# Filling the attention stage's idle TensorE time with 512-token blocks read back from DRAM instead of 288-token halves kept in SBUF

## The chip, the cores and the metric

The program runs on one core of a Trainium2 chip. A core has five engines, each with its own in-order instruction stream: TensorE (PE; its weight loads are shown as PEld), VectorE (DVE), ScalarE (ACT), GpSimd (POOL) and SyncE (SP), which here issues all DMAs. The metric is the device time of one execution in microseconds, lower is better. The kernel before took 1243.93 us (median of three executions, 1243.01 to 1246.9).

## The reference, cut to what matters

Three layers follow each other on a batch of 8 sequences of 576 tokens with 512 channels.

```python
# 1. attention over 32 pooled memories: 8 batches x 8 heads, phi [.., 576, 32]
a   = softmax(phi, over the 576 tokens' 32 memories)
k_m = einsum('bhsm,bhsd->bhmd', a, k);  v_m = the same with v
x   = softmax(q @ k_m.T / 8) @ v_m                 # [8, 576, 512]
# 2. mixer: tokens, then channels
h = relu(x.T @ w_tok1) @ w_tok2;   u = x + h.T     # w_tok1 576x256, w_tok2 256x576
x = u + relu(u @ w_ch1) @ w_ch2                    # w_ch1 512x1536, w_ch2 1536x512
# 3. four experts of causal attention (64 wide), top 2 of 4 by a gate, weighted sum
out = sum over e of gate[e] * softmax(mask(q_e @ k_e.T / 8)) @ v_e @ wo[e]
```

All results are float32. The mixer's weights come as 64-bit floats and are turned into 32-bit words on the chip.

## The kernel before, in words

Every large product is made from three passes over a high and a low part (`mm3`, line 93): a value x is split into hi, a rounded copy made by ACT, and lo = x - hi, made by DVE (`split`, line 100).

The first stage ("stage A", lines 197 to 578) does attention and the token mixer for 16 units, a unit being four heads of one batch. It is a software pipeline: in iteration t of the loop at line 540 the functions `s1a` ... `s4c` each work on another unit, from t+3 down to t. `s2k` (line 294) pools k and v with `kv` as its operand and writes `ks` and the values; `s4g`, `s4b` and `s4c` are the token mixer of unit t. `s4c` writes a result tile u, which ACT takes out of PSUM (line 472), and stores it to DRAM as `u_d` (line 475). The channel mixer's 1536 hidden channels are 12 chunks (`fc`) of 128. Chunks 0 to 2 are computed in stage A as fill between the pieces of the pipeline, 7 to 10 us of TensorE work for each iteration; they read u from the tile in SBUF (`u1`), in halves of 288 tokens, 16 halves in all. A half (`block_1`, line 188) is four splits, three `mm1_1` (12 matmuls each) and four `mm2_1` (9 matmuls each), whose sum is added to u and stored as `p_d`. What is not done when stage A ends is done at the head of the second stage.

The second stage ("stage B", lines 602 to 720) reads u back from `u_d` (tiles `ub`) in 9 blocks of 512 tokens, computes chunks 3 to 9, adds the stored `p_d` (tiles `pb`) and stores `x_d`. The third stage computes chunks 10 and 11 and the experts' attention. The 64-bit weights of a chunk come in two tensors; each is one DMA of 512 KB (tile `cst`), five DVE operations and two ACT operations (`f64_split`, line 111). `N1 + NP` chunks are prepared in stage A, the rest in stage B by `chload` (line 674). `go()` puts one such step at a time into the pipeline, `fill(k)` some pieces of fill.

The code's order is not the final one: a scheduler reorders the instructions of every engine when the program is built, so the order of each engine's instructions is shown below where it matters. At run time each engine goes through its stream in order and waits by semaphores. A DMA that SP issues waits on SP, and what stands behind it waits as well.

## Time and profile before

| | |
|---|---|
| three executions | 1243.01, 1243.93, 1246.9 us |
| profiled execution, its own time | 1243.78 us |
| its span, from first to last instruction | 1242.1 us |
| mean granted TensorE clock | 0.996 |
| PE, PEld busy | 1197.0 us, 1103.0 us |
| DVE, ACT, POOL busy | 703.5, 593.1, 382.5 us |
| DMA | 142.93 MB, 115 GB/s on average |

A profile has views: the page (busy shares, slices, the chain that ended last, costliest groups), stretches of time with each engine's busy time, groups of instructions of one form, the instructions in order of time, and DMA issues with their time to landing. Busy time of PE overstates its work, since a matmul's end is modelled and matmuls overlap; the distance between the starts of two neighbours is what one costs. In the list by time a bracket gives the idle time before an instruction and whose result ended it.

### The profile page before, as it was taken

How to read it: one execution, taken by the hardware profiler on the slowest of the kernel's cores; microseconds unless marked ns; L12 is line 12 of the kernel's file. 1: busy time of each engine (PE TensorE's matmuls, PEld its weight loads, DVE VectorE, ACT ScalarE, POOL GpSimd, SP SyncE). 2: the span in 40 equal slices, each digit the busy share in tenths (PEclk: the TensorE clock that was granted, in tenths of full speed). 3: DMA queues.
4: the chain of work that ended last, by engine and by line, in shares of the span. 5: the costliest groups of instructions: out<-in, count | busy, mean ns of one | idle time of the engine just before them, and what ended most of it. 6: DMA issues, size and time to landing. Idle time of an engine off the chain costs nothing. (4 is left out here: it accounts for less than half of the span.)

```text
span 1242.1 us, 22995 instructions
## 1 busy us (share of the span) xinstructions
PE 1197.0 (96%) x8460; PEld 1103.0 (89%) x8460; DVE 703.5 (57%) x1757; ACT 593.1 (48%) x1542; POOL 382.5 (31%) x588
## 2 busy tenths in 40 slices
PE   5799999999999999999999999999999999999997
PEld 4789999999999888888888888999999999998995
DVE  6877576776546743222222214776666766676754
ACT  3555364655534411111111113676676767675775
POOL 1443242433300142000000006446363627282322
PEclk9899999999999999999999999999999999999999
DMA  9886574645218455320321104222223323331421
GB/s 231 231 212 177 149 186 140 179 135 143 78 68 295 134 156 178 102 72 30 102 69 68 57 37 111 61 82 79 80 85 82 97 66 109 98 88 46 136 92 60
DMA packets 159615, 142.93 MB, mean 115 GB/s; under 512 B 73104, under 2 KB 128400, under 8 KB 159504
## 3 DMA queue, kind: packets, MB, share of 16 engines
q1 hardware_dynamic: 159504, 141.47, 39.3%
q8 instruction: 67, 1.10, 0.4%
q14 instruction: 44, 0.36, 0.1%
HBM read 90.05 MB, written 39.85 MB: 105 GB/s over the span
## 5 line engine op out<-in xcount | busy, mean ns | idle before, releaser
L627 DVE SCALAR_TENSOR_TENSOR hl<-h,hh 128x512 fp32r<-128x512 f32 x63 | 43.4, 691 | 225.7 <-ACT hh L626 225.6
L626 ACT ACTIVATE hh<-h 128x512 fp32r<-128x512 f32 x63 | 37.5, 597 | 255.3 <-PE h L98 255.3
L923 POOL TENSOR_TENSOR a<-a,cf 128x128 f32<-128x128 f32 (+3 forms) x128 | 88.0, 720 | 62.3 <-DVE cf L915 50.9
L98 PE MATMUL h<-uh,w1h 128*128 128x512 f32 x252 | 98.0, 390 | 0.4 <-DVE hl L627 0.4
L98 PE MATMUL h<-ul,w1h 128*128 128x512 f32 x252 | 98.1, 389 | 0.0
L98 PE MATMUL o<-hl,w2h 128*128 128x512 f32 x252 | 98.1, 389 | 0.0
L98 PE MATMUL o<-hh,w2l 128*128 128x512 f32 x252 | 98.0, 389 | 0.0
L98 PE MATMUL h<-uh,w1l 128*128 128x512 f32 x252 | 98.0, 389 | 0.0
L98 PE MATMUL o<-hh,w2h 128*128 128x512 f32 x252 | 88.9, 389 | 0.0
L867 DVE CUSTOM_DVE_ANT_0 ssb<-s,cmask 128x128 f32<-128x128 f32 (+2 forms) x144 | 69.3, 484 | 31.6 <-PE s L878 20.5
L389 POOL TENSOR_TENSOR at<-ssb,ssm 128x640 f32<-128x640 f32 x16 | 21.4, 1336 | 200.3 <-DVE ks L316 110.8
L880 ACT ACTIVATE a<-ssb,nb 128x128 f32<-128x128 f32 (+3 forms) x128 | 71.5, 559 | 13.8 <-DVE nb L867 8.8
L98 PE MATMUL g<-xl,qkh 128*128 128x288 f32 x256 | 76.4, 299 | 0.0
L98 PE MATMUL g<-xh,qkh 128*128 128x288 f32 x256 | 75.7, 301 | 0.2 <-DVE kk L803 0.2
L98 PE MATMUL g<-xh,qkl 128*128 128x288 f32 x256 | 75.6, 296 | 0.0
L729 POOL MEMSET cmask<- 128x640 f32 x1 | 0.6, 632 | 226.0 <-PE h L98 226.0
L780 POOL TENSOR_TENSOR xl<-p,xh 128x288 fp32r<-128x288 f32 x64 | 50.8, 809 | 45.1 <-ACT xh L779 45.1
L105 DVE TENSOR_TENSOR Bl<-t,Bh 128x512 fp32r<-128x512 f32 (+1 forms) x80 | 50.6, 635 | 18.8 <-ACT Bh L102 17.6
L98 PE MATMUL b<-uh,w1h 128*128 128x288 f32 x192 | 58.7, 306 | 0.0
L98 PE MATMUL b<-hh,w2h 128*128 128x288 f32 x192 | 58.4, 304 | 0.0
L98 PE MATMUL b<-hl,w2h 128*128 128x288 f32 x192 | 58.0, 302 | 0.0
L939 PE MATMUL t<-ident,a 128*128 128x128 f32 x320 | 55.7, 279 | 1.9 <-DVE Al L105 1.2
(261 smaller groups left out, 3998.9 us busy)
## 6 DMA issues: line engine op xcount, KB each, us to landing
cst<-in_moe_w_ch_dram SPq DMA_DIRECT2D x24, 512.0 KB, 4.7
u_d<-u SPq DMA_DIRECT2D x32, 288.0 KB, 2.2
p_d<-u SPq DMA_DIRECT2D x16, 576.0 KB, 3.3
ub<-u_d SPq DMA_DIRECT2D x9, 1024.0 KB, 5.2
pb<-p_d SPq DMA_DIRECT2D x36, 256.0 KB, 3.7
x_d<-pb SPq DMA_DIRECT2D x36, 256.0 KB, 2.4
u<-u_d SPq DMA_DIRECT2D x16, 576.0 KB, 4.3
p<-x_d SPq DMA_DIRECT2D x16, 576.0 KB, 4.1
```

Of the source, the lines that this page charges most:

```text
L98: PE.matmul(ps, lhsT=a, rhs=b, start=start and i == 0, stop=stop and i == len(seq) - 1)
L105: DVE.tensor_sub(lo, src, f(hi))
L389: POOL.tensor_mul(a_[:].rearrange("p j (h m) -> p j h m", h=4), s[:], sm[:, :, :, None].to_broadcast([128, 5, 4, M]))
L626: ACT.activation(hh[:], p[:], AF.Relu)
L627: DVE.scalar_tensor_tensor(hl[:], p[:], 0.0, f(hh[:]), op0=OP.max, op1=OP.subtract)
L729: POOL.memset(cmask[:], 0.0)
L780: POOL.tensor_sub(xl[b][:, c, ss], x_, f(xh[b][:, c, ss]))
L867: DVE.tensor_tensor_reduce(out=out, in0=p, in1=mask, scale=-scale, scalar=least, op0=OP.add, op1=OP.min, accum_out=acc)
L880: ACT.activation(a[:, aoff[c]:aoff[c] + W], s_[:, 0:W], AF.Exp, scale=-1.0, bias=nb[:, 0:1], accum_out=sm[:, c:c + 1])
L923: POOL.tensor_mul(x_, x_, cf[:, c:c + 1].to_broadcast([128, W]))
L939: PE.transpose(p[:, 128 * kc:128 * kc + 128], a[:, aoff[c] + 128 * kc:aoff[c] + 128 * kc + 128], ident[:])
```

## The change: what it does

The fill of stage A takes blocks of 512 tokens, 9 in all, instead of 16 halves of 288. It no longer reads u from SBUF: a block is loaded from `u_d` (`load_1`) once the unit that completes its 512 tokens has been stored, and its splits stand between the `mm2_1` of the block before. Fill starts at iteration 4 instead of 3, and a piece is given out for every second slot. The sum of chunks 0 to 2 is stored alone, by piece of 128 channels (tiles `po`), taken out of PSUM by ACT and DVE in turn; u is added to it in stage B by POOL, in `load_p`. One chunk's weights less are prepared in stage A and one more in stage B (`NP` 3), and the channel weights begin an iteration later. The masked values (`s2v`) are made one iteration later than the rest of `s2k`.

```diff
--- before.py
+++ after.py
@@ -130,7 +130,7 @@
         yield
 
 
-    N1, NP, N3 = 3, 4, 2
+    N1, NP, N3 = 3, 3, 2
     KM = KF - N3
     wch_ctx, b1_ctx, stg_ctx = ExitStack(), ExitStack(), ExitStack()
     wbm = wch_ctx.enter_context(tc.tile_pool(name="wbm", bufs=1, reuse_waits="tile"))
@@ -155,43 +155,66 @@
                                  l_[fc][:].rearrange("p c f -> p (c f)"), DM, wd)
 
 
-    u1, uh1, ul1, h1 = {}, {}, {}, {}
-
-    def half(j):
-        return slice(SH * (j % 2), SH * (j % 2) + SH)
-
-    def split_1(j, k0):
-        if k0 == 0:
-            uh1[j] = wk1.tile([128, KD, SH], F32R, name="uh1")
-            ul1[j] = wk1.tile([128, KD, SH], F32R, name="ul1")
-        split(uh1[j][:, k0, :], ul1[j][:, k0, :], u1[j // 2][:, k0, half(j)])
-
-    def mm1_1(j, fc):
-        p = ppb1.tile([128, SH], F32, name="b", bufs=2)
-        mm3(p[:], [((w1h[fc][:, kd, :], w1l[fc][:, kd, :]), (uh1[j][:, kd, :], ul1[j][:, kd, :]))
-                   for kd in range(KD)])
-        hh = wk1.tile([128, SH], F32R, name=f"hh{fc}")
-        hl = wk1.tile([128, SH], F32R, name=f"hl{fc}")
+    NBLK = NT // 512
+    ub1, uh1, ul1, h1 = {}, {}, {}, {}
+    units_out, split_out = -1, -1
+
+    def load_1():
+
+        k0 = len(ub1)
+        if k0 < NBLK and split_out >= k0 - 1 and units_out >= 2 * ((512 * k0 + 511) // S) + 1:
+            ub1[k0] = wk1.tile([128, KD, 512], F32, name="ub1")
+            SP.dma_start(ub1[k0][:], u_d[:, 512 * k0:512 * k0 + 512].rearrange("(c p) s -> p c s", p=128))
+
+    def split_1(k0, kd):
+        nonlocal split_out
+        if kd == 0:
+            uh1[k0] = wk1.tile([128, KD, 512], F32R, name="uh1")
+            ul1[k0] = wk1.tile([128, KD, 512], F32R, name="ul1")
+        split(uh1[k0][:, kd, :], ul1[k0][:, kd, :], ub1[k0][:, kd, :])
+        if kd == KD - 1:
+            split_out = k0
+            load_1()
+
+    def mm1_1(k0, fc):
+        p = ppb1.tile([128, 512], F32, name="b", bufs=2)
+        for i in range(2):
+            mm3(p[:], [((w1h[fc][:, kd, :], w1l[fc][:, kd, :]), (uh1[k0][:, kd, :], ul1[k0][:, kd, :]))
+                       for kd in range(2 * i, 2 * i + 2)], start=(i == 0), stop=(i == 1))
+            if i == 0:
+                yield
+        hh = wk1.tile([128, 512], F32R, name=f"hh{fc}")
+        hl = wk1.tile([128, 512], F32R, name=f"hl{fc}")
         ACT.activation(hh[:], p[:], AF.Relu)
         DVE.scalar_tensor_tensor(hl[:], p[:], 0.0, f(hh[:]), op0=OP.max, op1=OP.subtract)
-        h1[j, fc] = hh, hl
-
-    def mm2_1(j, c):
-        p = ppb1.tile([128, SH], F32, name="b", bufs=2)
-        mm3(p[:], [((w2h[fc][:, c, :], w2l[fc][:, c, :]), (h1[j, fc][0][:], h1[j, fc][1][:]))
+        h1[k0, fc] = hh, hl
+        yield
+
+    def mm2_1(k0, c):
+        p = ppb1.tile([128, 512], F32, name="b", bufs=2)
+        mm3(p[:], [((w2h[fc][:, c, :], w2l[fc][:, c, :]), (h1[k0, fc][0][:], h1[k0, fc][1][:]))
                    for fc in range(N1)])
-        u_ = u1[j // 2][:, c, half(j)]
-        DVE.tensor_add(u_, u_, p[:])
-        if c == KD - 1:
-            SP.dma_start(p_d[:, SH * j:SH * j + SH].rearrange("(c p) s -> p c s", p=128), u1[j // 2][:, :, half(j)])
-
-    def block_1(j):
-        for kd in range(KD):
-            yield split_1(j, kd)
+        o_ = wk1.tile([128, 512], F32, name="po1", bufs=2)
+        if c % 2:
+            DVE.tensor_copy(o_[:], p[:])
+        else:
+            ACT.activation(o_[:], p[:], AF.Copy)
+        SP.dma_start(p_d[128 * c:128 * c + 128, 512 * k0:512 * k0 + 512], o_[:])
+
+    def block_1(k0):
+        if k0 == 0:
+            while k0 not in ub1:
+                yield
+            for kd in range(KD):
+                yield split_1(k0, kd)
         for fc in range(N1):
-            yield mm1_1(j, fc)
+            yield from mm1_1(k0, fc)
+        while k0 + 1 < NBLK and k0 + 1 not in ub1:
+            yield
         for c in range(KD):
-            yield mm2_1(j, c)
+            if k0 + 1 < NBLK:
+                split_1(k0 + 1, c)
+            yield mm2_1(k0, c)
 
 
     with ExitStack() as sa:
@@ -227,7 +250,7 @@
         units = [(b, g) for b in range(B) for g in range(2)]
         NU = len(units)
         NR = 6
-        et, kmT, Vh, Vl, ah, al, pmc, est, kst, ssb, aTt, gt_, ht, pmx, Vd = ({} for _ in range(15))
+        et, kmT, Vh, Vl, ah, al, pmc, est, kst, ssb, aTt, gt_, ht, pmx, Vd, vmt = ({} for _ in range(16))
 
         def load_phi(n):
             b, g = units[n]
@@ -315,13 +338,16 @@
             kst[n] = ks
             DVE.scalar_tensor_tensor(ks[:], p[:, None, 0:64].to_broadcast([128, 2, 64]), r[:],
                                      kmask[:], op0=OP.mult, op1=OP.mult)
-            vm = wk_.tile([128, 64], F32, name="vm", bufs=1)
+            vm = wk_.tile([128, 64], F32, name="vm", bufs=2)
+            vmt[n] = vm
             ACT.activation(vm[:], p[:, 64:128], AF.Copy, scale=r[:])
             if n + 1 < NU:
                 load_kv(n + 1)
-            vmb = vm[:, None, :].to_broadcast([128, 4, 64])
-            h_ = wk_.tile([128, 4, 64], F32R, name="Vh", bufs=3)
-            l_ = wk_.tile([128, 4, 64], F32R, name="Vl", bufs=3)
+
+        def s2v(n):
+            vm = vmt.pop(n)
+            h_ = wk_.tile([128, 4, 64], F32R, name="Vh", bufs=2)
+            l_ = wk_.tile([128, 4, 64], F32R, name="Vl", bufs=2)
             Vh[n], Vl[n] = h_, l_
             vh = wk_.tile([128, 64], F32R, name="vh", bufs=1)
             vl = wk_.tile([128, 64], F32, name="vl", bufs=1)
@@ -332,7 +358,7 @@
             if n < NR:
                 Vd[n] = h_, l_
                 return
-            d_ = wk_.tile([128, 2, 4, 64], F32R, name="Vd", bufs=3)
+            d_ = wk_.tile([128, 2, 4, 64], F32R, name="Vd", bufs=2)
             Vd[n] = d_
             for i, x in enumerate((h_, l_)):
                 for c, o in ((0, 0), (1, 64)):
@@ -453,11 +479,9 @@
             b, g = units[n]
             x_, d_ = aTt.pop(n), Vd.pop(n)
             hh, hl = ht.pop(n)
-            if g == 0:
-                u1[b] = wk1.tile([128, KD, S], F32, name="u1", bufs=2)
             for c in range(2):
                 cs = slice(128 * c, 128 * c + 128)
-                u_ = u1[b][:, 2 * g + c, :]
+                u_ = wk_.tile([128, S], F32, name="us", bufs=2)
                 for hf in range(2):
                     ss = slice(SH * hf, SH * hf + SH)
                     pu = pp.tile([128, 512], F32, name="g", bufs=2)[:, 0:SH]
@@ -472,7 +496,7 @@
                     ACT.activation(u_[:, ss], pu, AF.Copy)
                     yield
                 r0 = 256 * g + 128 * c
-                SP.dma_start(u_d[r0:r0 + 128, b * S:(b + 1) * S], u_)
+                SP.dma_start(u_d[r0:r0 + 128, b * S:(b + 1) * S], u_[:])
 
         w1w, w2w = words(w_tok1), words(w_tok2)
 
@@ -530,16 +554,18 @@
             if 0 <= n < NU:
                 return fn(n, *args)
 
-        NJ = 2 * B
-        blocks = (piece for j in range(NJ) for piece in block_1(j))
-
-        def b1some(k):
-            for _ in range(k):
+        blocks = (piece for k0 in range(NBLK) for piece in block_1(k0))
+        due = 0
+
+        def fill(k):
+            nonlocal due
+            due += k * (t >= 4)
+            while due >= 2:
+                due -= 2
                 next(blocks, None)
 
         for t in range(-3, NU):
-            go = (lambda: wsome(1)) if t < -1 else behind if t < 3 else wsoon
-            fill = (lambda k: b1some(min(k, 1) if t >= NU - 2 else 2 * k if t == 4 else k)) if t >= 3 else (lambda k: None)
+            go = (lambda: wsome(1)) if t < 0 else behind if t < 4 else wsoon
             on(s1a, t + 3)
             on(s4a, t)
             fill(2)
@@ -552,6 +578,7 @@
             on(s3b, t + 1)
             fill(1)
             on(s2k, t + 2)
+            on(s2v, t + 1)
             go()
             fill(1)
             on(s4b, t)
@@ -573,6 +600,8 @@
             if c4:
                 for _ in c4:
                     pass
+            units_out = t
+            load_1()
         for _ in wc:
             pass
         stg_ctx.close()
@@ -598,7 +627,6 @@
         POOL.tensor_sub(ul2[j][:, kd, :], u2[j][:, kd, :], f(uh2[j][:, kd, :]))
 
 
-    NBLK = NT // 512
     with ExitStack() as sb:
         wk_ = sb.enter_context(tc.tile_pool(name="wkb", bufs=2, reuse_waits="tile"))
         wb2 = sb.enter_context(tc.tile_pool(name="wb2", bufs=1, reuse_waits="tile"))
@@ -646,6 +674,7 @@
         def load_p(n, c):
             pb[n, c] = wk_.tile([128, 512], F32, name="pb", bufs=4)
             SP.dma_start(pb[n, c][:], p_d[128 * c:128 * c + 128, 512 * n:512 * n + 512])
+            POOL.tensor_add(pb[n, c][:], pb[n, c][:], ub[n][:, c, :])
 
         def wcload():
             for i, w in enumerate((wq, wk)):
@@ -681,7 +710,7 @@
         for i, _ in enumerate(blocks):
             if i == 0:
                 load_u(1)
-            if i < 20:
+            for _ in range(1 + i % 2 if i < 20 else 0):
                 next(wcl, None)
         for kd in range(KD):
             split_u(0, kd)
```

**TensorE at the end of stage A.** `g<-aT,Vd` and `g<-t2h,...` are the last unit's `s4c`, `b<-` is fill, and `uh`, `ul` are the split parts of u. Before:

```order
L468 MATMUL g<-aT,Vd 128x288 x2
L98 MATMUL g<-t2h,hh 128x288
L98 MATMUL g<-t2l,hh 128x288
L98 MATMUL g<-t2h,hl 128x288
L98 MATMUL b<-hh_5125,w2h_617 128x288
L98 MATMUL b<-hl_5126,w2h_617 128x288
L98 MATMUL b<-hh_5125,w2l_618 128x288
L98 MATMUL b<-hh_5153,w2h_854 128x288
```

Now, where `uh_4541` and `ul_4542` are the split parts of the eighth block, tile `ub_4463`:

```order
L492 MATMUL g<-aT,Vd 128x288 x2
L98 MATMUL g<-t2h,hh 128x288
L98 MATMUL g<-t2l,hh 128x288
L98 MATMUL g<-t2h,hl 128x288
L98 MATMUL b<-uh_4541,w1h_454 128x512
L98 MATMUL b<-uh_4541,w1h_547 128x512
L98 MATMUL b<-ul_4542,w1h_454 128x512
L98 MATMUL b<-uh_4541,w1l_455 128x512
```

Before, 18 second products of a half already in SBUF follow the last unit, then the 36 first products of the next half (`uh_5264`), then stage B; now the eighth block's first products (24 matmuls, of chunks 0 and 1) follow at once, then stage B.

**SyncE at the same place.** Before, then now:

```order
L475 DMA u_d<-u_4914 128x576
L612 DMA ub<-u_d 128x4x512
L475 DMA u_d<-u_4914 128x576
L612 DMA ub<-u_d 128x4x512
L150 DMA cst<-in_moe_w_ch_dram 128x4x256
```

```order
L202 DMA p_d<-po_4615 128x512
L499 DMA u_d<-us 128x576 x2
L167 DMA ub_4463<-u_d 128x4x512
L640 DMA ub<-u_d 128x4x512 x2
L676 DMA pb<-p_d 128x512 x4
```

The eighth block's load stands right behind the last unit's stores and waits for their landing; the second stage's loads stand behind it.

**ScalarE at one block's load in the middle of stage A.** `us<-g` is the last eviction of a unit's `s4c`, `hh<-g` the eviction of the next unit's `s4b`, `uh_2960<-ub_2558` the four high parts of the fourth block. Now:

```order
L496 ACTIVATE us<-g 128x288
L201 ACTIVATE po_2974<-b 128x512
L406 ACTIVATE ssb<-ssb 128x640
L102 ACTIVATE gh<-g 128x256
L385 ACTIVATE qTb_116<-t 128x512
L343 ACTIVATE vm<-g,kr 128x64
L385 ACTIVATE qTb_116<-t 128x512
L102 ACTIVATE uh_2960<-ub_2558 128x512 x4
L425 ACTIVATE ahi<-at 128x512
L426 ACTIVATE ahi<-at 64x128
L128 ACTIVATE w1h_2427<-cy 128x512
L474 ACTIVATE hh<-g 128x512
```

Before, at such a place:

```order
L472 ACTIVATE u_3115<-g 128x288
L102 ACTIVATE aT<-t 64x64 x2
L102 ACTIVATE gh<-g 128x256
L380 ACTIVATE ssb<-ssb 128x640
L175 ACTIVATE hh_3710<-b 128x288
L359 ACTIVATE qTb_116<-t 128x512
L319 ACTIVATE vm<-g,kr 128x64
L448 ACTIVATE hh<-g 128x512
```

The four splits of a block, which need a DMA's data, now stand between `vm` and the eviction `hh<-g`; before, the splits read a tile in SBUF and stood elsewhere.

**VectorE early in stage A** (after the third unit's `ea`; `cy`, `cm`, `t2l` are steps of the weights' preparation). Before, then now:

```order
L129 TENSOR_TENSOR t2l<-cy,t2h 128x576
L105 TENSOR_TENSOR aT<-t,aT 128x512
L121 TENSOR_SCALAR cm<-cm 128x512
L124 TENSOR_SCALAR cy<-cst 128x512
L105 TENSOR_TENSOR aT<-t,aT 128x64
L125 SCALAR_TENSOR_TENSOR cm<-cm,cy 128x512
L124 TENSOR_SCALAR cy<-cst 128x512
L376 TENSOR_REDUCE smx<-s 128x20
L125 SCALAR_TENSOR_TENSOR cm<-cm,cy 128x512
```

```order
L129 TENSOR_TENSOR t2l<-cy,t2h 128x576
L105 TENSOR_TENSOR aT<-t,aT 128x512
L105 TENSOR_TENSOR aT<-t,aT 128x64
L402 TENSOR_REDUCE smx<-s 128x20
L405 TENSOR_TENSOR ssb<-s,smx 128x640
L411 TENSOR_REDUCE ssm<-ssb 128x20
```

The channel weights' steps (11 DVE operations up to the next `ks`) have left this place for the iterations behind it.

## Rows read from the trace of the kernel before

**Rows 1.** The page: busy time of each engine, share of the span, instructions.

```profile
PE 1197.0 (96%) x8460; PEld 1103.0 (89%) x8460; DVE 703.5 (57%) x1757; ACT 593.1 (48%) x1542; POOL 382.5 (31%) x588
```

**Rows 2.** Stretches: start:end, length, busy PE, PEld, DVE, ACT, POOL, PEclk, DMA.

```profile
44.30:64.20 19.90, 16.16 (x177) 15.49 (x176) 14.45 (x29) 10.49 (x23) 6.03 (x7) 0.83 0.69 188
64.20:79.80 15.60, 15.21 (x190) 14.96 (x189) 8.88 (x20) 9.64 (x24) 6.17 (x7) 1.00 0.84 215
79.80:102.10 22.30, 20.09 (x225) 19.22 (x226) 20.68 (x43) 12.41 (x31) 7.07 (x8) 1.00 0.72 194
...
238.70:260.80 22.10, 22.10 (x205) 21.74 (x204) 14.47 (x32) 11.32 (x30) 8.01 (x14) 1.00 0.57 159
```

**Rows 3.** PE starts: start us, duration us; fill of 288 columns, then 512 columns.

```profile
365.43 0.29 PE L98 MATMUL b<-uh,w1h 128*128 128x288 f32 x1
...
368.36 0.29 PE L98 MATMUL b<-ul,w1h 128*128 128x288 f32 x1
...
501.02 0.39 PE L98 MATMUL h<-ul,w1h 128*128 128x512 f32 x1
...
503.06 0.39 PE L98 MATMUL h<-ul,w1h 128*128 128x512 f32 x1
```

**Rows 4.** Groups by form: the fill's matmuls (count, busy us, mean ns, idle before).

```profile
L98 PE MATMUL b<-uh,w1h 128*128 128x288 f32 x192 | 58.7, 306 | 0.0
```

**Rows 5.** Two early stretches with VectorE's busy time and the clock (columns of rows 2).

```profile
31.60:50.00 18.40, 13.03 (x138) 11.86 (x138) 17.65 (x36) 11.09 (x23) 7.06 (x7) 1.00 0.95 258
50.40:57.20 6.80, 5.27 (x23) 5.30 (x24) 5.20 (x11) 3.29 (x9) 5.33 (x6) 0.50 1.07 252
```

**Rows 6.** TensorE's early waits, by time: idle before, and who ended it.

```profile
48.22 0.39 PE L98 MATMUL g<-Vh,gh 128*128 128x256 f32 x1 [1.27 <-DVE gl L105]
51.93 0.45 PE L345 MATMUL t<-ident,ks 128*128 128x128 f32 x1 [2.47 <-DVE ks L316]
...
84.58 0.38 PE L98 MATMUL g<-Vh,gh 128*128 128x256 f32 x1 [1.39 <-DVE gl L105]
```

**Rows 7.** The end of stage A by time: TensorE, ScalarE, SyncE.

```profile
377.61 0.30 PE L98 MATMUL b<-hh,w2h 128*128 128x288 f32 x1
...
377.81 0.41 ACT L472 ACTIVATE u<-g 128x288 f32<-128x288 f32 x1 [0.18 <-PE g L98]
...
378.25 0.32 SPq L475 DMA_DIRECT2D u_d<-u  x1
378.66 0.39 SPq L612 DMA_DIRECT2D ub<-u_d  x1
```

**Rows 8.** DMA issues: count, KB each, median us to landing; then tile `ub`.

```profile
u_d<-u SPq DMA_DIRECT2D x32, 288.0 KB, 2.2
...
ub<-u_d SPq DMA_DIRECT2D x9, 1024.0 KB, 5.2
...
DMA to landing us min/median/max: 5.0/5.2/9.9
```

**Rows 9.** Groups by form: a split of 512 columns, and a POOL operation.

```profile
L923 POOL TENSOR_TENSOR a<-a,cf 128x512 f32<-128x512 f32 x32 | 33.3, 1040 | 0.0
...
L105 DVE TENSOR_TENSOR ul<-ub,uh 128x512 fp32r<-128x512 f32 x36 | 24.0, 722 | 0.1
...
L102 ACT ACTIVATE uh<-ub 128x512 fp32r<-128x512 f32 x36 | 19.6, 622 | 0.0
```

**Rows 10.** A wait of TensorE in the third stage, and the stretch behind it.

```profile
1132.39 0.58 PE L98 MATMUL g<-vgh,xh 128*128 128x260 f32 x1 [1.88 <-DVE vhl L829]
...
1132.50:1135.80 3.30, 3.30 (x15) 3.30 (x16) 0.92 (x4) 1.13 (x5) 0.96 (x2) 0.50 0.43 161
1136.00:1141.00 5.00, 5.00 (x37) 4.83 (x36) 3.32 (x15) 2.56 (x8) 0.00 (x0) 1.00 0.01 2
```

**Rows 11.** ScalarE by time, in the middle of stage A.

```profile
235.05 0.41 ACT L472 ACTIVATE u<-g 128x288 f32<-128x288 f32 x1 [1.34 <-PE g L98]
...
242.25 0.31 ACT L319 ACTIVATE vm<-g,kr 128x64 f32<-128x64 f32 x1 [2.47 <-DVE ks L316]
```

**Rows 12.** Stage B: its first part (columns of rows 2), then VectorE by time.

```profile
400.00:450.00 50.00, 49.58 (x251) 42.37 (x250) 36.34 (x64) 17.08 (x30) 11.58 (x14) 1.00 0.50 155
...
509.78 0.69 DVE L627 SCALAR_TENSOR_TENSOR hl<-h,hh 128x512 fp32r<-128x512 f32 x1 [4.75 <-ACT hh L626]
```

## The prediction

> **What bounds the kernel now.** I read the page's busy times first: TensorE is busy 96% of the span, VectorE, the next one, 57% [rows 1]. Then the stretches of stage A, an iteration each: from 79.8 us on they last about 22 us, TensorE is busy all of it, VectorE 14.5 us and ScalarE 11.3 us [rows 2]. So TensorE's work sets the end, and any saving elsewhere counts only where TensorE waits. Next I looked for the places where it does wait, and for what the change puts in front of it. Early in stage A VectorE is busy 17.65 of 18.4 us, and the clock stands at half for 6.8 us [rows 5]; TensorE waits there for `gl` and for `ks` [rows 6]. At the border to stage B nothing waits today: TensorE goes on with the next half at 377.61 us while ScalarE takes out the last piece of u [rows 7].
>
> All sums are made against the profiled execution's own time, 1243.78 us: 1242.1 us of span and 1.7 us around it. It lies 0.15 us below the median of the three runs.
>
> **The change part by part.**
>
> *Width of the fill.* Before, the fill has 6 forms of 192 matmuls, 1152 in all [rows 4]; after, 9 blocks of 72, that is 648. In a run of 22 gaps without a wait a 288-wide matmul follows the one before after (368.36 - 365.43)/22 = 133.2 ns; a 512-wide one in stage B, over 9 gaps, after 226.7 ns [rows 3]. So 1152 x 0.1332 = 153.4 us becomes 648 x 0.2267 = 146.9 us: **-6.5 us**. All of it is on TensorE, hence on the path. The columns are the same in number (331,776); the saving is some 13 ns a matmul that does not depend on the width.
>
> The Trainium skill, page "TensorE: Matmul & The Clock Gate", section "Back-to-back issue gap", gives a single gap as N/2.4 + 2.5 ns. By that the two widths cost 122.5 and 215.8 ns, an estimate, the fill would go from 141.1 to 139.9 us, and the sum below would be 1253.5 us instead. The trace disagrees at both widths (133.2 and 226.7 ns), so I go by the trace.
>
> *Early relief of VectorE.* The channel weights begin one iteration later, and 11 DVE operations leave the stretch that ends at 50 us; the masked values go too. TensorE's waits of 1.27 and 2.47 us [rows 6] should go, and with them the reason for the half clock that follows at 50.4 us. At half clock 6.8 us hold 3.4 us of full-speed work, so that costs 3.4 us. Together 7.1 us. Late next: the work is only moved. VectorE's busy time over the three stretches from 44.3 to 102.1 us is 44.0 us, 14.7 each [rows 2], and the fill no longer covers iteration 3. TensorE's own work without fill is between 12.5 us (a later iteration's 22.1 us less 72 x 0.1332 = 9.6 us of fill) and the 15.2 us busy in the stretch without fill [rows 2]. I take 13.4, nearer the lower end because busy time overstates; two iterations then idle 1.3 us each, 2.6 us. Net **-4.5 us**. Ends: -8.5 if also the 1.39 us wait at 84.58 us goes [rows 6] and nothing idles; +4.4 if no wait goes and both iterations idle at 12.5 us of work.
>
> *The end of stage A.* This is the edit against the change. The eighth block holds tokens of the last unit, and on TensorE its first products stand right behind the last unit's `s4c`, with nothing between. Now the last eviction of u, its store, the store's landing, the load, its landing and the split must pass first. In the rows of before the store is issued at 378.25 us, 0.64 us after TensorE would go on (377.61) [rows 7]; a `u_d` store lands in 2.2 us, a 1024 KB load of `ub` in 5.2 us [rows 8]; that is 385.65. The first high part takes 0.62 us [rows 9]: 386.27, 8.7 us after 377.61. The low parts come at 0.72 us each [rows 9], which delays the second pass by about 0.3. So **+9.0 us**, all on the path. Ends: 8.5, with the load at its fastest (5.0) and no delay of the low part, and 13.7 with the slowest load seen, 9.9 us [rows 8]. SP's queue holds `ub` for stage B behind this load, so nothing of stage B can step in either.
>
> *The clock after that gap.* In the third stage a wait of 1.88 us was followed by 3.3 us at a granted 0.50, then 1.00 again [rows 10]; it cost half of 3.3, 1.65 us. The early stretch cost 3.4 [rows 5]. A gap of 9 us is longer than either wait, so I take the middle, **+2.5 us**; ends 0 and 3.4.
>
> *Read-backs in mid-stage.* Six blocks are loaded while the pipeline runs. ScalarE's four splits of each stand in its order between `vm` and `hh<-g`, after the eviction that completes the unit. From the end of that eviction (235.46) to the end of `vm` (242.56) 7.1 us pass [rows 11]; store and load take 2.2 + 5.2 = 7.4 us [rows 8], and a `p_d` store whose eviction takes about 0.7 us stands ahead on SP. So ScalarE waits some 0.4 to 1.1 us, and then four splits, 4 x 0.62 = 2.5 us [rows 9], stand ahead of `ahi` and `hh`, for which TensorE waits later. ScalarE has 10.8 us free in an iteration, which absorbs most. I take 0.5 us a block, 6 x 0.5 = **+3.0 us**. Ends: 0 when TensorE has fill in store at that point, and 6 x 1.8 = 11 when half of wait and splits together (3.6 us at most) comes through.
>
> *Start of stage B.* One chunk more is prepared there: two tensors, ten DVE operations. From 400 to 450 us VectorE has 13.7 of 50 us free, TensorE 0.4 [rows 12]. That should hide it, but where a weight operation stands ahead of `hl`, TensorE waits: **+1.0 us**. Ends: 0, and 5, half of ten operations near the 1.04 us row, the dearest 512-wide one shown [rows 9].
>
> *At nothing.* POOL's 36 additions of u are 36 x 1.04 = 37 us [rows 9], hidden beside POOL's 31% busy [rows 1], since `pb` is loaded well ahead of its use; with that cover gone each block's end would wait 1.04 us. VectorE loses 64 additions of 288 columns and gets 18 copies of 512; ScalarE gets 18. The extra loads, 9 of 1 MB, meet a DMA share of 0.57 [rows 2].
>
> Sum: 1243.8 - 6.5 - 4.5 + 9.0 + 2.5 + 3.0 + 1.0 = **1248.3 us**.
>
> **The rivals.**
>
> *Faster.* The early stretch gives back its whole 8.5 us and the gap costs the least, 8.5, with no clock loss and no waits in mid-stage: 1243.8 - 6.5 - 8.5 + 8.5 = 1237.3 us. For it: VectorE is nearly full exactly there [rows 5], and the later iterations have room on all other engines. Against it: a gap without a clock loss was not seen in rows 10. It decides once the early relief is worth over 5.7 us while the terms behind the gap stay near zero.
>
> *No change.* The gap is as long as forecast, but the clock holds and ScalarE's waits are absorbed, as is the extra chunk: 1243.8 - 6.5 - 4.5 + 9.0 = 1241.8 us. For it: ScalarE and VectorE have a third to a half of each iteration free [rows 2]. Against it: `hh` and `ahi` are short chains, and the splits stand right ahead of them.
>
> *Much slower.* ScalarE, in order, is blocked at each read-back, `hh` and the next products are late, and TensorE pays 11 instead of 3 us: 1256.3 us, and 1261.0 with the slowest load at the gap (13.7 instead of 9.0). For it: the read-back of 7.4 us is longer than the 7.1 us in hand. Against it: 0.3 us short is little. It decides from about 1 us lost a block.
>
> **How the numbers follow.** My forecast, a gap at the border that eats more than the width and the early relief bring, gets 0.45 and lies by itself between 1245.5 and 1254. Faster gets 0.20, no change 0.22, much slower 0.13. A measurement of this kernel can tell about 0.3% from no change, 1240.2 to 1247.7 us. Faster is its case: 0.20. Within: the no-change case and the lower edge of my own, 0.22 + 0.08 = 0.30. Slower: 0.37 + 0.13 = 0.50. The range runs from 1238 us, which leaves out the lower half of the faster case, to 1260 us, which leaves out the slowest landings. The likeliest case gives 1248.3.
>
> **What would show it.** In the profile after: right behind the last `s4c`, TensorE idle for about 9 us before its first matmul on the eighth block's `uh`, ended by ScalarE; the granted clock at 0.50 behind it; the fill's 512-wide matmuls 0.227 us apart; no waits for `gl` and `ks` near 48 and 52 us and no half clock there; ScalarE's `uh` of the fill ended by a DMA, and TensorE's waits for `hh` behind it. I am wrong if the gap is much below 8 us because the loads land sooner or something else stands there, if the early waits return with the moved weights, or if the mid-stage iterations keep to TensorE's own work and give back nothing.

## The result: slower by 1.2 to 1.5%, on the forecast side but past the range

The changed kernel took 1260.63 us (median of four executions, 1256.94 to 1263.38) against 1245.28 us, a ratio of 1.0123, 95% interval 1.0087 to 1.0158. In a second comparison it took 1263.08 to 1264.56 us in three executions against a median of 1245.59 us, 1.0151 (1.0134 to 1.0168); a fourth execution, slow as a whole (1342.05 us at a mean granted clock of 0.85), is left out. Forecast were 1248.3 us and a range that ended at 1260: the sign was right, the loss three to four times as large.

The profiled execution took 1256.94 us (span 1255.3 us), 13.2 us more than that of before, and its mean granted clock was 0.985 against 0.996. It is the fastest of the seven; the others took up to 7.6 us longer, so its trace shows the lower end of the loss. TensorE's busy time on the page hardly moved; what grew is idle time and time at the lower clock.

```profile
PE 1195.9 (95%) x7956; PEld 1071.5 (85%) x7956; DVE 696.7 (56%) x1662; ACT 596.8 (48%) x1511; POOL 436.6 (35%) x624
```

The end of stage A answers to [rows 7]. By time, on TensorE, ScalarE and SyncE:

```profile
367.11 0.29 PE L98 MATMUL g<-t2h,hl 128*128 128x288 f32 x1
376.01 1.22 PE L98 MATMUL b<-uh,w1h 128*128 128x512 f32 x2 [8.61 <-ACT uh L102]
...
367.44 0.41 ACT L496 ACTIVATE us<-g 128x288 f32<-128x288 f32 x1 [0.65 <-PE g L98]
...
375.33 1.15 ACT L102 ACTIVATE uh<-ub 128x512 fp32r<-128x512 f32 x2 [6.45 <-DMA ub<-u_d]
...
367.88 0.32 SPq L499 DMA_DIRECT2D u_d<-us  x1
370.01 0.37 SPq L167 DMA_DIRECT2D ub<-u_d  x1
```

The store is issued at 367.88 us, the load 2.13 us later, and the first split begins 5.32 us after that. TensorE idles for 8.61 us; 9.0 were forecast. The stretches behind it and early in the program (start:end, length, busy time of PE, PEld, DVE, ACT, POOL, granted clock, DMA share, GB/s) show the clock:

```profile
29.00:44.00 15.00, 10.16 (x55) 9.34 (x59) 11.52 (x19) 6.14 (x15) 6.80 (x7) 0.54 0.95 252
...
80.00:85.00 5.00, 3.69 (x16) 3.39 (x17) 5.00 (x9) 4.38 (x11) 2.83 (x4) 0.66 1.12 325
...
376.00:381.20 5.20, 5.19 (x12) 4.09 (x13) 5.20 (x9) 5.09 (x10) 0.00 (x0) 0.50 1.05 387
...
382.00:432.00 50.00, 50.00 (x220) 41.06 (x219) 32.12 (x53) 18.17 (x32) 8.67 (x4) 1.00 0.45 157
```

Behind the gap TensorE runs 5.2 us at half clock, 2.6 us lost. From 382 us on it is busy without a pause, so the chunk that stage B prepares more costs nothing. The early half clock of [rows 5] (6.8 us from 50.4 us on) did not go: it lies between 29 and 44 us now and is longer, and a second one follows at 80 us, where the fill begins.

TensorE's waits from 60 to 360 us (what waited, for whom: us in total, times, longest):

```profile
PE b L98 <- DVE po L199: 2.2, 1, 2.2
PE b L98 <- ACT po L201: 1.9, 1, 1.9
PE g L98 <- DVE hl L475: 1.8, 1, 1.8
PE t L382 <- DVE pmc L291: 1.6, 1, 1.6
PE b L98 <- ACT uh L102: 1.4, 1, 1.4
```

Three of these are the fill's own, 5.5 us. Around the second, ScalarE by time:

```profile
255.72 2.19 ACT L102 ACTIVATE uh<-ub 128x512 fp32r<-128x512 f32 x4 [1.37 <-DMA ub<-u_d]
257.82 0.58 ACT L201 ACTIVATE po<-b 128x512 f32<-128x512 f32 x1
```

ScalarE waits 1.37 us for the read-back, does four splits, and only then takes a finished sum out of PSUM; TensorE, at 258.45 us, had waited 1.87 us for that bank. The wait came as in the prediction, but what stood behind it was the fill's own eviction. At the first place ScalarE had waited only 0.15 us for the read-back; there it is VectorE, which makes three low parts of the next block before it copies a finished sum out of PSUM. VectorE, then TensorE, by time:

```profile
122.51 3.24 DVE L105 TENSOR_TENSOR ul<-ub,uh 128x512 fp32r<-128x512 f32 x3
125.68 0.68 DVE L199 COPY po<-b 128x512 f32<-128x512 f32 x1
...
126.41 0.50 PE L98 MATMUL b<-hh,w2h 128*128 128x512 f32 x1 [2.17 <-DVE po L199]
```

Two starts of the fill, ten gaps apart at full clock, answer to [rows 3]:

```profile
381.49 0.39 PE L98 MATMUL b<-uh,w1h 128*128 128x512 f32 x1
...
383.75 0.39 PE L98 MATMUL b<-uh,w1l 128*128 128x512 f32 x1
```

The distance is 0.226 us, as in stage B before: the width itself came as read.

### The profile page after: what moved, and what is told of

Its sections match the earlier page's. It is cut to its first block, busy times and chain, and to the rows that moved or that the text cites. A ratio compares the mean times of both kernels' runs of the same rounds, so it can differ in the third digit from the quotient of the medians.

```text
span 1255.3 us, 21992 instructions
## 1 busy us (share of the span) xinstructions
PE 1195.9 (95%) x7956; PEld 1071.5 (85%) x7956; DVE 696.7 (56%) x1662; ACT 596.8 (48%) x1511; POOL 436.6 (35%) x624
## 4 chain that ended last, share of the span: by engine, by line
PE 85%; DMA 4%; DVE 4%; ACT 2%; issue 1%; SPq 1%; POOL 1%; ACTq 0%; DVEq 0%; POOLq 0%
PE g L98 30%; PE h L98 14%; PE o L98 14%; PE b L98 11%; PE y L1014 4%; PE s L907 3%; PE t L968 3%; PE s L399 2%; DMA ub<-u_d 2%; PE s L929 1%; DMA cst<-in_moe_w_tok_dram 1%; PE g L323 1%; DMA u_d<-us 1%; DMA cst<-in_moe_w_ch_dram 1%; PE g L492 1%
## 5 line engine op out<-in xcount | busy, mean ns | idle before, releaser
L677 POOL TENSOR_TENSOR pb<-pb,ub 128x512 f32<-128x512 f32 x36 | 49.4, 1402 | 241.2 <-DMA pb<-p_d 241.0
L105 DVE TENSOR_TENSOR ul<-ub,uh 128x512 fp32r<-128x512 f32 x72 | 56.0, 833 | 11.4 <-ACT uh L102 11.4
L1021 POOL TENSOR_TENSOR yl<-yt,yh 128x256 fp32r<-128x256 f32 x32 | 23.7, 740 | 107.1 <-ACT yh L1020 102.8
L98 PE MATMUL b<-uh,w1h 128*128 128x512 f32 x108 | 45.1, 421 | 11.8 <-ACT uh L102 10.0
L98 PEld LDWEIGHTS o<-hl,w2h 128*128 128x128 f32 x252 | 47.3, 188 | 9.9
```

What stands on the lines that cost most here:

```text
L98: PE.matmul(ps, lhsT=a, rhs=b, start=start and i == 0, stop=stop and i == len(seq) - 1)
L105: DVE.tensor_sub(lo, src, f(hi))
L677: POOL.tensor_add(pb[n, c][:], pb[n, c][:], ub[n][:, c, :])
```

## The experiments

Theory A: most of the loss is the border, a wait and a half clock behind it. Theory B, against A: what covers the border is missed elsewhere, and little is gained. Theory C: the read-backs in mid-stage hold up evictions, and half clock follows those waits. Its rival: the coarser fill itself leaves TensorE without work. Ratios are to the kernel before, run on the same chip; the edits shown are cut to their core.

**The changed kernel again** (no edit).

> The changed kernel once more, as the yardstick of this chip. All theories: ratio to the kernel before between 1.009 and 1.016 (11 to 20 us).

Measured 1.0151 (1.0134 to 1.0168).

**The border taken away.**

```diff
+    def kx(k0):
+        return k0 if k0 < 7 else k0 - 2
-        if ... units_out >= 2 * ((512 * k0 + 511) // S) + 1:
+        if ... units_out >= 2 * ((512 * kx(k0) + 511) // S) + 1:
-            SP.dma_start(ub1[k0][:], u_d[:, 512 * k0:512 * k0 + 512] ...)
+            SP.dma_start(ub1[k0][:], u_d[:, 512 * kx(k0):512 * kx(k0) + 512] ...)
```

> As the changed kernel, but the eighth and ninth block read the tokens of the sixth and seventh, which lie stored long before, so nothing of the fill waits for the last unit (the chunks 0 to 2 of those 1024 tokens are then wrong). The work of every engine is the same. Theory A: 10 to 12 us faster than the changed kernel, no wait at the border. Theory B: under 4 us faster.

Measured 1.0049 (1.0031 to 1.0068), which is 12.7 us less than the changed kernel beside it (1.0151); against the first comparison's 1.0123 it is 9.2 us. Its clock is at full there:

```profile
366.00:372.00 6.00, 6.00 (x34) 5.28 (x33) 0.69 (x1) 1.42 (x3) 0.00 (x0) 1.00 0.35 130
```

So theory A holds for what the border costs, and 0.5% of loss is left elsewhere.

**The border covered with work held back:** 36 second products of the seventh block stand behind the last unit's `s4c`, and the splits behind their evictions.

```diff
+        if k0 == 6:
+            for c in range(KD):
+                with tc.issue_after(last_4c):
+                    mm2_1(k0, c)
```

> As the changed kernel, but the 36 second products of the seventh block (36 x 0.227 = 8.2 us) stand behind the last unit's s4c on TensorE, and the splits behind them on ScalarE and VectorE, so that they cover the read-back. Theory A (the border costs 8.6 us of wait and 2.4 us of half clock, and the rest of the loss lies elsewhere): 8 to 11 us faster than the changed kernel, ratio to the kernel before about 1.002 to 1.005; TensorE waits under 1 us at the border and the clock stays at full. Theory B (the products are only moved, and TensorE waits in the last two iterations for the work that they covered there): under 4 us faster.

Measured 1.0171 (1.0153 to 1.0188): nothing gained. TensorE, then ScalarE, by time:

```profile
383.81 0.80 PE L98 MATMUL b<-uh,w1h 128*128 128x512 f32 x1 [7.17 <-ACT uh L111]
...
382.65 0.60 ACT L212 ACTIVATE po<-b 128x512 f32<-128x512 f32 x1 [5.30 <-DMA p_d<-po]
```

Neither theory had this. The third eviction needs one of two `po` buffers, whose store stands in SyncE's queue behind 3 MB of loads; ScalarE waits 5.30 us for it, and the splits stand behind. The cover was there, and the queue took it back.

**The border filled with products that nobody reads.**

```diff
+            with tc.issue_after(last_4c):
+                for i in range(36):
+                    PE.matmul(p[:], lhsT=w2h[2][:, 0, :], rhs=h1[6, 2][0][:], start=True, stop=True)
```

> As the changed kernel, with 36 more products on TensorE (36 x 0.227 = 8.2 us), which nothing reads, in the wait at the border. If the half clock behind the wait comes from TensorE's idle time: the wait for ScalarE falls to about 0.5 us, the end of the read-back stays where it is, the clock is at full behind it, and the kernel is 2.4 us faster than the changed one, ratio about 1.013. If it comes from something else: half clock behind it all the same, no gain, ratio 1.015.

Measured 1.0101 (1.0078 to 1.0124), against 1.0123 and 1.0151 of the changed kernel in its two comparisons. The stretches of the extra products and of the 5.2 us behind them:

```profile
369.00:377.50 8.50, 8.15 (x36) 6.39 (x35) 4.38 (x8) 2.04 (x5) 0.00 (x0) 1.00 0.67 227
377.60:382.80 5.20, 5.20 (x22) 3.98 (x23) 5.20 (x9) 5.11 (x10) 0.00 (x0) 1.00 1.05 388
```

With the idle time filled the clock stays at full: 22 matmuls in 5.2 us, where the changed kernel has 12. The half clock behind the border is a consequence of the idle time before it. The trace shows this; the ratios put the gain at 2.7 us by the first comparison and 6.2 by the second, too far apart to size it.

**Evictions ahead of the splits,** without the border and, with 34 products covering it, in the whole kernel. In both, the second stage's first two loads of u stand behind the store of the seventh block's second piece.

```diff
         for c in range(KD):
-            if k0 + 1 < NBLK:
-                split_1(k0 + 1, c)
             yield mm2_1(k0, c)
+        while k0 + 1 < NBLK and k0 + 1 not in ub1:
+            yield
+        for c in range(KD if k0 + 1 < NBLK else 0):
+            split_1(k0 + 1, c)
```

> As the kernel whose eighth and ninth block read the tokens of the sixth and seventh (chunks 0 to 2 of 1024 tokens wrong), and in every block the evictions of the four second products now stand ahead of the next block's splits on ScalarE and VectorE. Theory C (in the middle of stage A the splits, which wait for the read-back, hold up the evictions behind them; TensorE waits 2 us for a bank at two places and runs 3.4 us at half clock after each): 8 to 10 us faster than without this edit, so 0.996 to 0.999 of the kernel before, and no waits of TensorE for an eviction of the fill between 100 and 330 us. Rival (what is left of the loss without the border is spread over the iterations, by lack of fill): under 3 us faster, ratio 1.002 to 1.005.

> The changed kernel, computing all of it, with the evictions ahead of the next block's splits in every block; 34 of the seventh block's second products then stand behind the last unit's s4c, and the second stage's first two loads of u stand behind the store of its second piece. Theory A and C together: the border's wait falls from 8.6 us to under 2, the half clocks in mid-stage go, about 16 to 20 us faster than the changed kernel, 0.997 to 1.002 of the kernel before. Rival (the border's wait is only moved, as the first try at covering it left 7.2 us of wait, by the stores of the pieces behind the loads in SyncE's queue): ratio 1.006 to 1.012.

Measured 1.0094 (1.0062 to 1.0126) and 1.0104 (1.0071 to 1.0138). The first is a miss for theory C: it is no faster than without the edit (1.0049). The second is as the rival had it. But the first run does not settle theory C. In its profiled execution (1253.55 us, against a median of 1258.1) the waits for the fill's evictions between 100 and 330 us are gone and the clock is at full, as theory C had it: TensorE idles 3.6 us there instead of 6.8. What was won is lost again at the border, where a copy waits for the landing of a `po` store and a half clock follows. The stretch in mid-stage, then VectorE, TensorE and the stretch at the border:

```profile
100.00:330.00 230.00, 226.37 (x1875) 203.87 (x1874) 148.45 (x273) 130.40 (x309) 92.83 (x148) 1.00 0.65 188
...
371.77 0.69 DVE L210 COPY po<-b 128x512 f32<-128x512 f32 x1 [2.35 <-DMA p_d<-po]
...
372.51 0.80 PE L98 MATMUL b<-uh,w1h 128*128 128x512 f32 x1 [3.19 <-DVE po L210]
...
371.90:378.70 6.80, 6.19 (x14) 4.73 (x15) 6.80 (x8) 3.93 (x8) 4.21 (x3) 0.50 1.05 395
```

In the whole kernel, ScalarE and then TensorE in mid-stage:

```profile
258.87 0.66 ACT L128 ACTIVATE cm<-cst 128x512 f32<-128x512 f32 x1 [2.31 <-DMA cst<-in_moe_w_ch_dram]
259.43 0.57 ACT L209 ACTIVATE po<-b 128x512 f32<-128x512 f32 x1
259.91 0.62 ACT L111 ACTIVATE uh<-ub 128x512 fp32r<-128x512 f32 x1
...
260.58 0.80 PE L98 MATMUL b<-uh,w1h 128*128 128x512 f32 x1 [2.62 <-ACT uh L111]
```

Here the order changed and the wait changed its name: ScalarE now waits for a weights' load, and TensorE 2.62 us for the split. At this place the order of evictions and splits was not all that held TensorE up; what the order costs in mid-stage was not measured by itself.

**No read-back waits for a unit.** Every block reads the first 512 tokens.

```diff
-        if ... units_out >= 2 * ((512 * k0 + 511) // S) + 1:
+        if ... units_out >= 1:
-            SP.dma_start(ub1[k0][:], u_d[:, 512 * k0:512 * k0 + 512] ...)
+            SP.dma_start(ub1[k0][:], u_d[:, 0:512] ...)
```

> As the changed kernel, but every block of the fill reads the first 512 tokens, which lie stored from the start (chunks 0 to 2 are wrong for all other blocks). The loads, splits and products are the same in number and size, only none waits for a unit's store. Theory C' (the read-back's waits, on SyncE's queue, ScalarE and TensorE, with the half clock behind them, are the loss in mid-stage; the places moved when evictions were put first, the waits did not go): no border, no waits of the fill between 100 and 360 us, 1239 to 1243 us against 1245, ratio 0.995 to 0.998. Rival (the coarser fill itself, at half the rate and in larger pieces, leaves TensorE without work): as without the border alone, ratio 1.003 to 1.007.

Measured 1.0003 (0.9987 to 1.0020): 0.46% less than without the border alone, about 5.7 us, so the mid-stage read-backs do cost. The result lies between theory C' (0.995 to 0.998) and its rival (1.003 to 1.007). TensorE's waits of this run from 60 to 110 us point to the rest:

```profile
PE b L98 <- ACT uh L102: 2.4, 1, 2.4
PE g L98 <- DVE hl L475: 1.8, 1, 1.8
```

The first block still has to wait until two units are stored.

**The first block too.** All blocks read an input, so that fill can begin as soon as its weights are ready.

```diff
+        if ... units_out >= 0:
+            SP.dma_start(ub1[k0][:], q[0] ... [0:DM * 512] ...)
```

> As the changed kernel, but every block of the fill reads 512 tokens' worth of an input (chunks 0 to 2 are wrong), so that the first block too is there before the fill begins; with stored tokens the first load came 4 us before its products and TensorE waited 2.4 us, with a half clock before and behind. If the late start of the fill is what eats the width's saving of 4 us (with every block reading the first tokens the ratio was 1.0003): 3 to 5 us faster than that, 0.996 to 0.998. Rival (the saving of the width is not there at all, or is eaten elsewhere): 0.999 to 1.002.

Measured 0.9935 (0.9911 to 0.9958), 1236.42 us: faster than expected. The first product of the fill, in this run, in the changed kernel and in the kernel before:

```profile
56.73 0.40 PE L98 MATMUL b<-uh,w1h 128*128 128x512 f32 x1
```

```profile
81.31 1.22 PE L98 MATMUL b<-uh,w1h 128*128 128x512 f32 x2 [1.36 <-ACT uh L102]
```

```profile
67.17 0.38 PE L98 MATMUL b<-uh,w1h 128*128 128x288 f32 x1
```

With the data at hand the fill starts 24.6 us earlier than in the changed kernel, and 10.4 us earlier than in the kernel before. The two runs differ by 0.0068, 8.5 us (an uncertainty of about 0.003 by the two intervals). Part of it shows from 60 to 110 us, in the run before this one and in this one:

```profile
60.00:110.00 50.00, 44.53 (x498) 41.34 (x497) 37.48 (x70) 28.20 (x64) 18.87 (x22) 0.93 0.82 231
```

```profile
60.00:110.00 50.00, 47.64 (x545) 44.18 (x544) 37.66 (x70) 26.97 (x64) 19.30 (x24) 1.00 0.85 236
```

TensorE idles 3.1 us less, and the clock is at full instead of 0.93.

**The early part alone,** on the kernel before: weights and masked values an iteration later, the fill unchanged.

```diff
-    N1, NP, N3 = 3, 4, 2
+    N1, NP, N3 = 3, 3, 2
-            go = (lambda: wsome(1)) if t < -1 else behind if t < 3 else wsoon
+            go = (lambda: wsome(1)) if t < 0 else behind if t < 4 else wsoon
+            on(s2v, t + 1)
```

> The kernel before with the other part of the change alone: channel weights one iteration later, one chunk more prepared in the second stage, masked values one iteration later; the fill stays as it was. By the prediction's step (early relief -4.5 us, the chunk +1.0): about 1240 us against 1243.8, ratio 0.997. By the trace of the changed kernel (the stretch up to 150 us gained nothing; a half clock of 13.7 us took the place of one of 6.8 us): within 1.5 us of the kernel before, ratio 0.999 to 1.001.

Measured 0.9980 (0.9965 to 0.9994), about 2.5 us faster (0.7 to 4.4), between the two. The expectation took the whole -4.5 us; but its 2.6 us of idle iterations come from the fill's later start, which this run does not have. Without them the prediction's terms make it 6.1 us faster. The same with four chunks in stage A:

> The kernel before with the channel weights and the masked values one iteration later and nothing else: four chunks are still prepared in stage A (the run with three measured 0.998). If the chunk moved to the second stage costs the 1.0 us of the prediction: 0.997. If moving it also relieves the end of stage A or costs nothing: 0.998 to 0.999.

Measured 0.9985 (0.9973 to 0.9997). The chunk's move costs nothing that can be told. Either version beats both kernels, by little.

**The early start of the weights put back** into the changed kernel (`t < -1`, `t < 3`).

> The changed kernel with the channel weights started as early as before (from the second-last iteration ahead of the first unit on), all else as changed. By the prediction's step (the later start relieves VectorE early, worth 4.5 us): 3 to 5 us slower than the changed kernel, ratio to the kernel before 1.016 to 1.020. By the trace of the changed kernel (no gain up to 150 us): within 2 us of it, ratio 1.010 to 1.015.

Measured 1.0167 (1.0145 to 1.0189), inside the range of the prediction's step and outside the other. But the changed kernel has 1.0151 (1.0134 to 1.0168), the intervals overlap, and the run decides nothing.

**The early clock held up** in the early part alone, by products that nobody reads.

```diff
+                for _ in range(3 * k):
+                    PE.matmul(p[:, 0:128], lhsT=ident[:], rhs=ident[:], start=True, stop=True)
```

> The kernel before with the early part of the change alone (which measured 0.998 and ran at half clock from 31 to 45 us), and 33 products of 128 columns more on TensorE in each of three early iterations, which nothing reads. If the half clock there costs time: full clock from 25 to 50 us and 2 to 4 us faster, ratio 0.994 to 0.996. If VectorE bounds that stretch whatever the clock: full clock and within 1 us of 0.998. If the products get in the way: slower, 1.000 or more.

Measured 1.0011 (0.9999 to 1.0024). The stretch from 31 to 45 us with the extra products, then without:

```profile
31.00:45.00 14.00, 13.15 (x171) 12.41 (x164) 10.65 (x19) 7.17 (x15) 5.86 (x7) 1.00 0.90 225
```

```profile
31.00:45.00 14.00, 10.23 (x60) 9.51 (x64) 9.80 (x16) 6.52 (x15) 6.81 (x7) 0.51 0.92 237
```

The clock is at full and the kernel no faster; its ratio is the one set for products that get in the way. What the half clock costs can still be read: ScalarE's first eviction of u begins at 54.47 us with the clock held up and at 54.45 us without. Up to there half clock cost nothing that can be told. That the extra products cost time behind it fits the ratio, but was not tried.

## Why the prediction was right in sign and wrong in size

*Border and clock: right.* 9.0 + 2.5 us were forecast; the wait was 8.61 us and the half clock lost 2.6. Taking the border away brought 12.7 us by the runs beside each other (1.0151 less 1.0049), 9.2 by the first comparison.

*Width: right in kind.* The fill's products follow each other after 0.226 us, as counted. With its data at hand from the start the changed kernel is 8.1 us faster than before; the width's 6.5 and the 2.5 of the early part alone make 9.0.

*The step that failed* is "Early relief of VectorE", net -4.5 us, and in it first the 7.1 us. With no border, and no block but the first waiting for a unit, the prediction's terms leave -6.5 - 4.5 + 1.0 = -10.0 us; that run measured 1.0003, +0.4 us (-1.6 to +2.5). The early part alone, where the relief stands without the fill's later start, brought 2.5 us where these terms had 6.1 (7.1 less the 1.0 of the chunk). The waits of [rows 6] did shrink in the changed kernel, to 0.84 us for `gl` and none for `ks` near 52 us, but a wait of 1.82 us for `hl` at 65 us is new (2.52 us in the early part alone). The half clock was counted as 3.4 us over 6.8 us in which TensorE was busy for 5.27 [rows 5], which makes 2.6 at most. It came earlier instead of going, and there it costs next to nothing: the first eviction of u begins at 54.26 us in the changed kernel and at 53.93 us in the run without read-back waits, whose clock is at full from 29 to 44 us.

*The start of the fill,* 2.6 us of the same step, was priced by the iteration number in the code. What decided was when the data are there. Before, a half's first split needs one piece of 128 channels and stands right behind the first eviction of u; now one load brings all pieces of a block, and it waits until two units are stored. ScalarE before, then SyncE in the changed kernel:

```profile
55.45 0.44 ACT L102 ACTIVATE uh<-u 128x288 fp32r<-128x288 f32 x1
```

```profile
75.25 0.37 SPq L167 DMA_DIRECT2D ub<-u_d  x1
```

The first product stands at 81.31 us instead of 67.17, so the stretch from 64.2 to 79.8 us, which the prediction read as one without fill, held some. It was little: up to 81.31 us the kernel before has done 17 fill products, 17 x 0.133 = 2.3 us. By the last eviction of the fourth unit the changed kernel has caught up, with 43 wide products done (9.7 us) against 73 narrow ones (9.7 us). The changed kernel, then the kernel before:

```profile
112.01 0.41 ACT L496 ACTIVATE us<-g 128x288 f32<-128x288 f32 x1 [0.74 <-PE g L98]
```

```profile
114.92 0.41 ACT L472 ACTIVATE u<-g 128x288 f32<-128x288 f32 x1 [1.68 <-PE g L98]
```

So the early stretch as a whole, relief less late start, gained 2.9 us in this execution and 0.8 in that of the run without the border (the same eviction at 114.14 us, with the same fill done), where 4.5 were forecast. The 8.5 us between the run at 1.0003 and the run at 0.9935 are what a fill with its data from the start would bring: that one has done 24 wide products (5.4 us) by 81 us, which the kernel before has not either. They are not what the change lost against the kernel before.

*Read-backs in mid-stage: mis-sized.* Forecast 3.0 us with ends 0 and 11, measured 5.7 by the runs (1.0049 less 1.0003). In the traces TensorE, busy without a pause before, idles 6.5 us from 110 to 360 us (0.9 in the run without read-back waits). The kernel before, then the changed one:

```profile
110.00:360.00 250.00, 250.00 (x2262) 245.70 (x2261) 164.50 (x341) 131.91 (x341) 83.85 (x142) 1.00 0.50 141
```

```profile
110.00:360.00 250.00, 243.50 (x1883) 217.92 (x1883) 155.85 (x273) 133.77 (x316) 91.89 (x142) 1.00 0.58 169
```

The mechanism, ScalarE held by the read-back, was seen, but not six times: of the two waits of some 2 us for an eviction, one has it, and at the other the splits stand ahead on VectorE. The clock stayed at full behind both in this execution; in the run without the border half clock followed each. The rival "much slower" named this mechanism with 1256.3 us; its price of 11 us was above what the runs show, and its total came near for other reasons.

*Start of stage B, and what was priced at nothing: right* for the changed kernel: TensorE is busy 50.00 of 50 us there. POOL's additions took 1.40 us each instead of 1.04 and hid all the same. In the runs without the border TensorE idles 1.7 to 2.3 us between 360 and 430 us, which was not forecast.

From run to run the measured steps are 0.4 + 5.7 + 12.7 = 18.8 us, against -10.0 + 3.0 + 11.5 = 4.5. They give 1.0151 by construction, and each carries some 3 us of uncertainty. Of the 14 us between them 10 stand in the first step. The early relief accounts for 3.6 of these (6.1 less 2.5); the rest stays open. Whether half clocks have a part in it, which differ from execution to execution of the same instructions (last section), was not tried.

## What to carry to other kernels

Before work that fills an engine's idle time is given a new source of data, mark three places: when the first piece can start, what is behind its wait in each in-order queue, and whether the last piece needs the last result. The price at each is the whole round trip, here 2.1 us of store, 5.3 of load and 0.6 of split, unless other work stands between; and cover that ends in a store can be undone by the loads queued ahead of that store. Where TensorE is the bound, count the half clock that may follow a wait as part of its price; early in this kernel, where TensorE waits for other engines anyway, it cost next to nothing. Before a version with its data at hand is taken as the measure of a late start, see when the kernel before started.

## What the runs showed of the hardware

The same wait of TensorE draws a half clock in one execution and none in another. Up to 350 us the changed kernel and the run without the border have the same instructions in the same order on TensorE, ScalarE and VectorE, and in both TensorE waits for the fill's eviction near 260 us, 1.87 us in the one and 2.52 in the other. Behind it, in that order:

```profile
257.70:260.70 3.00, 2.25 (x12) 1.90 (x13) 3.00 (x5) 2.20 (x6) 0.87 (x2) 1.00 1.07 213
```

```profile
261.50:264.50 3.00, 2.19 (x5) 1.81 (x6) 3.00 (x6) 2.10 (x5) 0.82 (x1) 0.56 1.06 228
```

Near 127 us the wait is 2.17 us in both, and again half clock follows in the second alone. By the last eviction of the fourteenth unit the two executions are 5.2 us apart:

```profile
329.81 0.41 ACT L496 ACTIVATE us<-g 128x288 f32<-128x288 f32 x1
```

```profile
334.96 0.41 ACT L499 ACTIVATE us<-g 128x288 f32<-128x288 f32 x1
```

At the start of the third stage the changed kernel and the kernel before both wait 1.21 us for `ul`; behind it the clock stands at 0.50 in the changed kernel and at full in the kernel before. The waits, of the changed kernel and then of the kernel before:

```profile
764.60 0.40 PE L98 MATMUL g<-ul,w1h 128*128 128x288 f32 x1 [1.21 <-POOL ul L627]
```

```profile
753.00 0.40 PE L98 MATMUL g<-ul,w1h 128*128 128x288 f32 x1 [1.21 <-POOL ul L598]
```

A stretch behind each, in the same order:

```profile
767.00:770.00 3.00, 2.80 (x10) 2.60 (x11) 0.82 (x2) 0.45 (x2) 2.96 (x6) 0.50 0.98 328
```

```profile
755.20:758.20 3.00, 2.61 (x17) 2.29 (x17) 1.18 (x3) 0.66 (x2) 2.76 (x6) 1.00 0.97 316
```

What decides whether a half clock follows was not tried.
